# Hash bits on four column quarters, placed by small transfers, in a hash attention kernel

## The chip, the cores and the metric

The kernel runs on one core of a Trainium2 chip. The metric is device microseconds from start to end of one execution of the whole program, the median over several runs. The engines named below are TensorE (PE in the profile, PEld for its weight loads), VectorE (DVE), ScalarE (ACT), GpSimd (POOL) and SyncE (SP, which here only issues transfers).

## The reference

Hash attention over 4 batches x 8 heads, 768 tokens, 64 columns a head, then a feed-forward block. A query sees only the keys whose six hash bits equal its own:

```python
q_bits = (np.einsum('bhsd,dk->bhsk', q, proj) > 0).astype(np.int64)
k_bits = (np.einsum('bhsd,dk->bhsk', k, proj) > 0).astype(np.int64)
q_bucket = np.sum(q_bits * powers, axis=-1)
k_bucket = np.sum(k_bits * powers, axis=-1)
mask = q_bucket[:, :, :, None] == k_bucket[:, :, None, :]
scores = scale * np.matmul(q, k.transpose(0, 1, 3, 2))
scores = np.where(mask, scores, -1000000000.0)
...
attn = attn / (np.sum(attn, axis=-1, keepdims=True) + 1e-09)
return np.matmul(attn, v).astype(np.float32)
...
h = x @ w_in
sp = np.maximum(h, 0.0) + np.log1p(np.exp(-np.abs(h)))
g = h * erf(sp)
return (g @ w_out).astype(np.float32)
```

The feed-forward block has 3072 rows, 512 columns in and out and 2048 inside. All of it is float32.

## The kernel before

The program has two stages: `attention` and `feed_forward`. A third part, `general`, does attention without assumptions on the size of the scores; it is behind a branch at the end and isn't executed with these inputs.

**Pairs, halves, blocks.** Attention works on 16 pairs of heads (`NPAIR`). Two heads of 64 columns fill 128 partitions. `fetch` (L330) brings q, k (transposed, 64 rows a head) and v of a pair with six transfers from SP, into buffers for three pairs. The 768 queries of a pair are two halves of 384 (`HS`). A half `h` has two `score` steps `n`, each over three blocks of 128 keys. One block (L529) is four matmuls for the two heads: 64 rows of bf16 hash signs times hash signs, then 64 rows of float32 k times q, summed in the same bank. The signs of the keys are weighted by 2^100 and a constant row takes the full match off again, so that a pair of tokens with differing bits gets a sum so low that its exponential is 0.

**The signs now.** `hash_bits` (L353) multiplies q and k by the projection: four float32 matmuls of 128 rows by 64 columns, q into partitions 0 to 63 and k into 64 to 127, one pair of matmuls for each half of 384 tokens. The projection `proj_sb` holds head a's six columns at column 0 and head b's at column 32 (`QR`). `sign_bits` (L366) takes the sign with one ACT instruction of 128 x 768, `spread_bits` (L379) writes the weighted key signs twice with DVE, once for each head, with weights that are zero in the other head's rows, and `double_bits` (L390) copies the query signs to the lower partitions with DVE. The tiles `qb` and `kb` have two buffers each. Pair 0 does this in two halves ahead of the loop (`take_bits`, L394).

**After the scores.** `exponential` (L543) goes to ACT, with three buffers in PSUM (`big`) shared by scores and hash bits. `sum_keys` (L590) sums the exponentials over blocks with DVE. `weigh` (L602) multiplies them by v, `divisor` (L635) sums over partitions: four matmuls of 32 columns side by side, 192 columns each. `keep_divisor` (L648) and `leave` (L659) copy both results out with ACT. Then a chain of small transfers on SP inverts and applies the sums, once for each pair: `spread` (zd, L678), `gather` (zc, L685), `invert` with DVE, `ungather` (rd, L703), `widen` (r, two transfers, L713), `normalise` with DVE (L721) and `send` (xs, L727). The tile x, which `leave` writes and `send` reads, has two buffers, and so has the tag that z and r share. On SP one queue takes all of this in order, with the loads of a later pair among it.

Beside that the weights of the feed-forward block are fetched by POOL (L439) and split into float32 with ACT and DVE (L453 to L515), 32 pieces through the whole stage.

**What sets the order.** Each engine executes its instructions in the order in which they are emitted. For attention, `arrange` (L118) makes this order: every step is an `Op` with an engine, an assumed cost in us, a rank, the steps it comes after, and `late`, an assumed delay until other engines see the result. `arrange` plays the steps through with these numbers and takes, at each point, the step that can start first. The order of TensorE is a fixed chain written out by hand (L786 to L793): for each half the next two scores, then, after every even half `h`, the bits of pair `h // 2 + 1`, the divisor of the half before, and two `weigh` steps. The waits themselves follow from which instruction reads or writes which tile.

Of the kernel before, what the change touches and what calls it, by code (L numbers as in the profile page):

```python
# [54 lines left out]
F32 = mybir.dt.float32  # L55
BF16 = mybir.dt.bfloat16
# [7 lines left out]
P = 128  # L64
# [129 lines left out]
def kernel(  # L194
# [33 lines left out]
    misc = ctx.enter_context(tc.tile_pool(name="misc", bufs=1, space=PSUM))  # L228
    small = ctx.enter_context(tc.tile_pool(name="small", bufs=3))
    QR = 32  # L230
    WARM = 7
    proj_sb = const.tile([P, 2 * QR], F32, name="proj_sb")
    weight = const.tile([P, 2], F32, name="weight")
    ones = const.tile([P, D], F32, name="ones")
    sgn = const.tile([P, 1], F32, name="sgn")
    tiny2 = const.tile([P, 1], F32, name="tiny2")
# [18 lines left out]
        )  # L255
    row = const.tile([P, 1], F32, name="row")
    nc.gpsimd.dma_start(out=row, in_=bucket)
    steps = const.tile([P, 5], F32, name="steps")
    for c, (end, factor) in enumerate(
        (  # L260
            (NBIT, NBIT + 1.0),
            (NBIT + 1, -float(NBIT)),
            (QR, -1.0),
            (QR + NBIT, NBIT + 1.0),
            (QR + NBIT + 1, -float(NBIT)),
        )
    ):
        nc.vector.tensor_scalar(
            out=steps[:, c : c + 1],
            in0=row,  # L270
            scalar1=float(end),
            scalar2=factor * BIG,
            op0=ALU.is_lt,
            op1=ALU.mult,
        )
    nc.vector.reduce_sum(out=weight[:, 0:1], in_=steps[:, 0:2], axis=AX.X)
    nc.vector.reduce_sum(out=weight[:, 1:2], in_=steps[:, 2:5], axis=AX.X)
    nc.vector.memset(sgn, -(2.0**-27))
    nc.vector.memset(tiny2, TINY * TINY)
    for j, (c, _) in enumerate(ERF_Q):  # L280
# [72 lines left out]
    def hash_bits(d, big, halves=(0, 1)):  # L353
        if halves[0] == 0:
            d["bits"] = big("bits")
        for half in halves:
            for n, what in enumerate("qk"):
                nc.tensor.matmul(  # L358
                    out=d["bits"][n * D : n * D + D, half, 0:HS],
                    lhsT=proj_sb,  # L360
                    rhs=d[what][:, half * HS : (half + 1) * HS],
                    start=True,
                    stop=True,
                )

    def sign_bits(d, bitp, cols):  # L366

        if cols.start == 0:
            for what in ("qb", "kb"):
                d[what] = bitp.tile([P, S], BF16, name=what, tag=what)  # L370
        nc.scalar.activation(
            out=d["qb"][:, cols].rearrange("p (h s) -> p h s", s=HS),
            in_=d["bits"][:, cols.start // HS : cols.stop // HS, 0:HS],
            func=AF.Sign,
            scale=2.0**100,
            bias=sgn[:, 0:1],
        )
# [12 lines left out]
    def double_bits(d, cols):  # L390

        nc.vector.tensor_copy(out=d["qb"][D:P, cols], in_=d["qb"][0:D, cols])

    def take_bits(d, bitp, halves=(0, 1)):  # L394
        cols = slice(halves[0] * HS, (halves[-1] + 1) * HS)
        sign_bits(d, bitp, cols)
        for ab in (1, 0):
            spread_bits(d, cols, ab)
        double_bits(d, cols)

    def attention():
        NS = NPAIR * 4
        with (
            tc.tile_pool(name="load", bufs=3) as load,
            tc.tile_pool(name="bitp", bufs=2) as bitp,
            tc.tile_pool(name="ep", bufs=1) as ep,
            tc.tile_pool(name="sums", bufs=2) as sums,
            tc.tile_pool(name="xst", bufs=2) as xst,
# [5 lines left out]
            def big(name):  # L414
                return psum.tile([P, 2, 512], F32, name=name, tag="big", bufs=3)

            junk = ep.tile([P, HS], BF16, name="junk")
            NE = 3 * GC
            e_all = ep.tile([P, NE, 2, HS + 1], F32, name="e_all")
# [335 lines left out]
                )  # L755
            for half in range(2):
                hash_bits(pairs[0], big, (half,))
                take_bits(pairs[0], bitp, (half,))

            NH = NPAIR * 2  # L760
            ops = []
# [9 lines left out]
                chain.append((fn.__name__,) + args)  # L771

            def bits_of(i):
                hash_bits(pairs[i], big)

            def sign_of(i):
                sign_bits(pairs[i], bitp, slice(0, S))

            def weigh_bits(i, ab):
                spread_bits(pairs[i], slice(0, S), ab)  # L780

            def copy_bits(i):
                double_bits(pairs[i], slice(0, S))

            chain = []
            order = [("score", 0)]  # L786
            for h in range(NH):
                order += [("score", n) for n in (2 * h + 1, 2 * h + 2) if n < NS]
                if h % 2 == 0 and h // 2 + 1 < NPAIR:
                    order.append(("bits", h // 2 + 1))  # L790
                if h >= 1:
                    order.append(("divisor", h - 1))
                order += [("weigh", 2 * h), ("weigh", 2 * h + 1)]  # L793
            slots = []
            for what, n in order:
                if what == "score":
                    i = n // 4
                    after = tuple(("weigh_bits", i, ab) for ab in range(2)) + (("copy_bits", i),)
                    for c in range(GC):
                        free = (slots[-3],) if len(slots) >= 3 else ()  # L800
                        pe(score, (n, c), 0.82, after + free)
                        slots.append(("exponential", n, c))
                elif what == "bits":
                    pe(bits_of, (n,), 1.34, (("start_pair", n), slots[-3]))
                    slots.append(("sign_of", n))
                elif what == "divisor":
                    pe(divisor, (n,), 0.42, (("sum_keys", n, last_sum(n)), ("keep_divisor", n - 1)))
                else:
                    h = n // 2
                    after = (("exponential", n, GC - 1),)  # L810
                    if n % 2 == 0:
                        after += (("leave", h - 1), ("leave_plain", (h - 1) // 2))
                    pe(weigh, (n,), 2.02, after)
# [40 lines left out]
            for i in range(NPAIR):  # L854
                n = 4 * i
                if i:
                    op(
                        start_pair,
                        (i,),
                        "SP",  # L860
                        3.6,
                        (0, n - 6),
                        (("weigh", n - 9), ("bits_of", i - 1))
                        + tuple(("measure", i - 3, m, half) for m in range(2) for half in range(2)),
                        late=3.5,
                    )
                    op(sign_of, (i,), "ACT", 0.88, (0, n - 2, 9), (("bits_of", i), ("score", n - 5, 2)))
                    for ab in (1, 0):
                        op(weigh_bits, (i, ab), "DVE", 0.43, (0, n - 2, 1), (("sign_of", i),))
                    op(  # L870
                        copy_bits,
                        (i,),
                        "DVE",
                        0.35,
                        (0, n - 2, 2),
                        (("weigh_bits", i, 0), ("weigh_bits", i, 1)),
                    )
                for m in range(2):
                    for half in range(2):
                        op(  # L880
                            measure,
                            (i, m, half),
                            "ACT",
                            0.5,
                            (1, 2 * i + 2, 2 + m, half),
                            (("start_pair", i), ("score", n, 0)),
                        )
                if i == NPAIR - 1:
                    continue
                op(spread, (i,), "SP", 0.4, (0, n, 0), (("keep_divisor", 2 * i + 1),), late=3.0)  # L890
                op(gather, (i,), "SP", 0.35, (0, n, 1), (("spread", i),), late=4.5)
                op(invert, (i,), "DVE", 0.4, (0, n + 8, 3), (("gather", i),))
                op(ungather, (i,), "SP", 0.35, (0, n, 2), (("invert", i),), late=3.0)
                op(
                    widen,
                    (i,),
                    "SP",
                    1.1,
                    (0, n, 3),
                    (("ungather", i), ("send", i - 1)),  # L900
                    late=6.5,
                )
                op(normalise, (i,), "DVE", 0.95, (0, n + 8, 4), (("widen", i), ("leave", 2 * i + 1)))
                op(send, (i,), "SP", 0.35, (0, n, 4), (("normalise", i),), late=2.2)
            for n in range(len(pieces)):
                op(
                    fetch_weights,
# [46 lines left out]
    def general():  # L954

        with (
# [13 lines left out]
            for i in range(NPAIR):  # L970
                d = fetch(i, load)
                b, j = divmod(i, JP)
                hash_bits(d, big)
                take_bits(d, bitp)
                x = ep.tile([P, S], F32, name="x", tag="x")
                for ab in range(2):
                    rows = slice(ab * D, ab * D + D)
# [701 lines left out]
```

## Time and profile before

| | |
|---|---|
| median of 3 runs | 933.58 us (931.9 to 934.86) |
| profiled execution: its own time | 934.86 us |
| profiled execution: its span | 932.9 us |
| mean granted TensorE clock | 0.997 of full |
| instructions | 12993 |
| attention | from the start to about 339 us |
| exponentials, L543, 192 instructions | 149.1 us of ACT, 819 ns each |
| score matmuls, float32, L529 | 156.6 us of PE, 486 ns each, side by side |
| hash bit matmuls, L358, 128 instructions | 51.2 us by single durations, side by side |
| small transfers zd, zc and rd | 6 KB each, 15 or 16 times |
| bytes moved | 80.92 MB, 87 GB/s on the mean |

Span and run time differ by 2 us that lie around the profiled instructions. A float32 matmul shows up as two instructions, one for each pass, and matmuls on different rows or columns of the array run side by side, so that single durations add up to more than the time they take. What a block of matmuls costs is better read from the distance between the starts of neighbouring blocks in the chain of waits.

Idle time of an engine is listed beside the instruction that ended it, with what released it. In the rows of SP (SPq), the times are those of issuing; a row's idle time before it is a wait.

### The profile page before, as it was taken

To read this page: it belongs to the slowest core of one execution; us is meant where nothing else is said; L and a number is where in the kernel's file an instruction comes from. 1 tells how busy PE (TensorE), PEld (TensorE's weight loads), DVE (VectorE), ACT (ScalarE), POOL (GpSimd) and SP (SyncE) were. 2 spreads that over 40 slices of the span, in tenths; PEclk is the share of its full clock that TensorE was granted. 3 is DMA by queue.
4 is the path that set the end of the run, shared out by engine and by line. 5 is a ranking of instruction groups with operands and counts; after the bars stand their busy time and mean duration, and the time that the engine had idled before them with its cause. 6 is when DMAs were issued, how large, how long until landed. Compare 5 with 4: busy or idle time off the path is not lost.

```text
span 932.9 us, 12993 instructions
## 1 busy us (share of the span) xinstructions
PE 916.8 (98%) x5003; PEld 661.9 (71%) x5003; DVE 829.7 (89%) x1041; ACT 771.0 (83%) x1002; POOL 17.4 (2%) x35
## 2 busy tenths in 40 slices
PE   8999999999999999999999999999999999999996
PEld 3444444444444458888888888888888888888885
DVE  4999998999888997899999889998899789988995
ACT  5888787768876838999998998899989997899891
POOL 0000000000000000000000000000000000000000
PEclk9999999999999999999999999999999999999998
DMA  8365455576654322010212012210221111001211
GB/s 198 99 158 147 132 148 139 147 200 165 147 149 131 97 103 97 1 46 34 80 68 79 34 46 69 80 34 34 79 78 36 34 65 49 34 34 46 68 35 48
DMA packets 61398, 80.92 MB, mean 87 GB/s; under 512 B 33296, under 2 KB 46224, under 8 KB 61328
## 3 DMA queue, kind: packets, MB, share of 16 engines
q1 hardware_dynamic: 56672, 64.08, 23.9%
q0 software_dynamic: 4352, 15.73, 5.6%
q8 instruction: 41, 0.67, 0.3%
q10 hardware_dynamic: 304, 0.20, 0.1%
q14 instruction: 29, 0.24, 0.1%
HBM read 64.07 MB, written 15.93 MB: 86 GB/s over the span
## 4 chain that ended last, share of the span: by engine, by line
PE 85%; DVE 7%; DMA 4%; ACT 2%; issue 1%; SPq 0%; DVEq 0%; ACTq 0%
PE M L1238 30%; PE X L1098 27%; PE st L529 11%; PE av L602 9%; PE M L1098 3%; PE bits L358 2%; DMA xs<-x 1%; ACT e_all L543 1%; DVE x_sum L590 1%; PE z_ps L635 1%; DVE x L590 1%; DMA zd<-z 1%; DMA zc<-zd 1%; DVE x L721 1%; DMA r<-rd 1%
## 5 line engine op out<-in xcount | busy, mean ns | idle before, releaser
L1165 DVE SCALAR_TENSOR_TENSOR e<-w,e 128x1024 f32<-128x1024 f32 x144 | 173.4, 1221 | 5.8 <-ACT w L1161 3.0
L1161 ACT ACTIVATE w<-w,cq 128x1024 f32<-128x1024 f32 x144 | 160.7, 1143 | 1.9
L543 ACT ACTIVATE e_all<-st 128x768 f32<-128x768 f32 x192 | 149.1, 819 | 11.3 <-PE st L529 11.3
L529 PE MATMUL st<-q,k 64*128 64x384 f32 x768 | 156.6, 486 | 0.0
L1238 PE MATMUL M<-w_out_sb,h 128*128 128x256 f32 x576 | 140.2, 380 | 0.4 <-DVE h L1180 0.4
L602 PE MATMUL av<-e_all,v 128*64 128x385 f32 (+1 forms) x768 | 131.1, 490 | 0.0
L1098 PE MATMUL X<-x,w_in_sb 128*128 128x256 f32 x512 | 121.2, 380 | 0.0
L1238 PEld LDWEIGHTS M<-w_out_sb,h 128*128 128x128 f32 x576 | 109.3, 190 | 15.9 <-DVE h L1180 1.1
L1098 PEld LDWEIGHTS X<-x,w_in_sb 128*128 128x128 f32 x512 | 97.1, 190 | 13.8 <-ACT h L1116 0.6
L602 PEld LDWEIGHTS av<-e_all,v 128*64 128x64 f32 x768 | 52.4, 136 | 67.2 <-issue 65.4
L1238 PE MATMUL M<-wt,S 128*128 128x256 f32 x384 | 93.4, 379 | 0.4 <-DVE S L1195 0.4
L529 PEld LDWEIGHTS st<-q,k 64*128 64x128 f32 x768 | 69.1, 190 | 32.8 <-issue 32.1
L1098 PE MATMUL X<-x_sum,w_sum 128*128 128x256 f32 x344 | 81.7, 380 | 1.8 <-ACT h L1116 1.8
L1238 PEld LDWEIGHTS M<-wt,S 128*128 128x128 f32 x384 | 72.9, 190 | 10.7 <-DVE S L1195 0.8
L1098 PEld LDWEIGHTS X<-x_sum,w_sum 128*128 128x128 f32 x344 | 65.1, 190 | 12.0 <-ACT h L1116 3.3
L1116 ACT COPY h<-X 128x512 f32<-128x512 f32 x85 | 49.0, 577 | 22.3 <-PE X L1098 21.4
L1142 DVE SCALAR_TENSOR_TENSOR w<-w,e 128x1024 f32<-128x1024 f32 x48 | 58.4, 1221 | 9.6 <-ACT w L1137 9.3
L529 PE MATMUL st<-qb,kb 64*128 64x384 bf16 x384 | 63.7, 327 | 3.3 <-ACT e_all L543 3.2
L1180 DVE TENSOR_TENSOR h<-h,e 128x1024 f32<-128x1024 f32 x48 | 58.0, 1221 | 6.1 <-ACT e L1176 5.9
L659 ACT COPY x<-av 128x384 f32<-128x384 f32 x32 | 15.3, 478 | 57.4 <-DMA xs<-x 28.8
L1156 ACT ACTIVATE w<-e 128x1024 f32<-128x1024 f32 x48 | 50.4, 1050 | 13.3 <-DVE e L1152 13.0
L1152 DVE TENSOR_TENSOR e<-e,w 128x1024 f32<-128x1024 f32 x48 | 57.5, 1219 | 2.7 <-ACT e L1148 2.6
(117 smaller groups left out, 1421.0 us busy)
## 6 DMA issues: line engine op xcount, KB each, us to landing
wt<-wt SPq DMA_DIRECT2D x24, 768.0 KB, 4.3
raw<-in_w_out_dram POOLq DMA_DIRECT2D x16, 512.0 KB, 3.9
raw<-in_w_in_dram POOLq DMA_DIRECT2D x14, 512.0 KB, 4.2
v<-in_v_dram SPq DMA_DIRECT2D x32, 192.0 KB, 4.5
xs<-x SPq DMA_DIRECT2D x16, 384.0 KB, 2.4
q<-in_qkT_dram SPq DMA_DIRECT2D x30, 192.0 KB, 3.4
k<-in_qkT_dram SPq DMA_DIRECT2D x30, 192.0 KB, 4.2
r<-rd SPq DMA_DIRECT2D x30, 192.0 KB, 3.5
```

The costliest lines, as they stand in the source:

```text
L529: nc.tensor.matmul(out=st[:, ab, 0:HS], lhsT=d["k" + src][rows, keys], rhs=d["q" + src][rows, cols], start=(part == 0), stop=(part == 1),)
L543: nc.scalar.activation(out=e[:, :, 0:HS], in_=st[:, :, 0:HS], func=AF.Exp, scale=scale)
L602: nc.tensor.matmul(out=d["av"][rows, 0:w], lhsT=d["v"][:, g * GC + c, rows], rhs=e[:, ab, 0:w], start=(g == 0 and c == 0), stop=(g == 1 an ...
L1098: nc.tensor.matmul(out=d[where][:, u, :], lhsT=a[:, kc, f : f + P], rhs=b[:, kc, :], start=(first and u == 0 and kc == 0), stop=(last and ...
L1116: nc.scalar.copy(out=quarter(p, q), in_=st[p][where])
L1142: nc.vector.scalar_tensor_tensor(out=w, in0=w, scalar=-1.0, in1=st[p]["e", v], op0=ALU.add, op1=ALU.subtract)
L1152: nc.vector.tensor_tensor(out=s, in0=s, in1=st[p].pop(("w", v)), op=ALU.subtract)
L1156: nc.scalar.activation(out=z, in_=st[p]["s", v], func=AF.Square)
L1161: nc.scalar.activation(out=q, in_=z, func=AF.Square, bias=cq[:, j : j + 1])
L1165: nc.vector.scalar_tensor_tensor(out=s, in0=st[p].pop(("q", v, j)), scalar=ERF_Q[j][1], in1=s, op0=ALU.add, op1=ALU.mult,)
L1180: nc.vector.tensor_tensor(out=h, in0=h, in1=st[p].pop(("s", v)), op=ALU.mult)
L1238: nc.tensor.matmul(out=banks[name][:, sub, :], lhsT=a[:, u, sub * P : (sub + 1) * P], rhs=b[:, u, :], start=(c == 0 and k == 0), stop=(c = ...
```

## The change

For pairs 1 to 15 the hash bits are computed by four matmuls of 32 columns side by side (`proj_q`, where head b's columns stand at column 16, `QB`): the two halves of q in partition quarters 0 and 1, those of k in quarters 2 and 3, in one PSUM bank. One ACT instruction of 128 x 384 takes the signs into one tile `sg`, of which there is one. One DVE instruction weights the key half of it. Then eight transfers on SP (`place_bits`), each of 7 rows by 384 columns of bf16, copy the six signs and the constant row of each head and half into `qb` and `kb`, whose other rows are zero. `qb` and `kb` are two fixed buffers each, used in turn; the ones with number 1 are cleared by POOL at the start, those with number 0, which pair 0 fills in the old way, by two POOL steps (`clean`) after pair 0's last score.

In TensorE's chain the bits of a pair move: they come after the scores of odd halves, half a pair earlier than before, and those of pair 1 come right after the second score step. The steps' assumed costs and their conditions change with it. Some small DVE instructions at the start make `proj_q` and the new weights. Pair 0 and `general` keep the old way.

```diff
+    QB = QR // 2
+    proj_q = const.tile([P, QR], F32, name="proj_q")
+    weight_q = const.tile([P, 1], F32, name="weight_q")
...
+    nc.vector.memset(proj_q, 0.0)
+    for ab in range(2):
+        rows = slice(ab * D, ab * D + D)
+        nc.vector.tensor_copy(
+            out=proj_q[rows, ab * QB : ab * QB + NBIT],
+            in_=proj_in[rows, ab * NBIT : (ab + 1) * NBIT],
+        )
+    nc.vector.reduce_sum(out=weight_q, in_=steps[:, 5:8], axis=AX.X)
+    nc.vector.tensor_tensor(out=weight_q, in0=weight_q, in1=weight[:, 0:1], op=ALU.add)
+    nc.vector.tensor_copy(out=weight_q[D + QR : P, :], in_=weight_q[D : D + QR, :])
...
+            sg = bitp.tile([P, HS], BF16, name="sg")
+            spare = {
+                (what, n): bitp.tile([P, S], BF16, name=f"{what}{n}")
+                for n in range(2)
+                for what in ("qb", "kb")
+            }
+            for what in ("qb", "kb"):
+                nc.gpsimd.memset(spare[what, 1], 0.0)
...
             def bits_of(i):
-                hash_bits(pairs[i], big)
+                d = pairs[i]
+                d["bits"] = big("bits")
+                for n, what in enumerate("qk"):
+                    for half in range(2):
+                        row = (2 * n + half) * QR
+                        nc.tensor.matmul(
+                            out=d["bits"][row : row + QR, 0, 0:HS],
+                            lhsT=proj_q,
+                            rhs=d[what][:, half * HS : (half + 1) * HS],
+                            start=True,
+                            stop=True,
+                        )
 
             def sign_of(i):
-                sign_bits(pairs[i], bitp, slice(0, S))
-
-            def weigh_bits(i, ab):
-                spread_bits(pairs[i], slice(0, S), ab)
-
-            def copy_bits(i):
-                double_bits(pairs[i], slice(0, S))
+                nc.scalar.activation(
+                    out=sg,
+                    in_=pairs[i].pop("bits")[:, 0, 0:HS],
+                    func=AF.Sign,
+                    scale=2.0**100,
+                    bias=sgn[:, 0:1],
+                )
+
+            def weigh_bits(i):
+                nc.vector.tensor_scalar(
+                    out=sg[D:P, :],
+                    in0=sg[D:P, :],
+                    scalar1=weight_q[D:P, 0:1],
+                    scalar2=None,
+                    op0=ALU.mult,
+                )
+
+            def place_bits(i):
+                d = pairs[i]
+                for n, what in enumerate(("qb", "kb")):
+                    d[what] = spare[what, i % 2]
+                    for half in range(2):
+                        for ab in range(2):
+                            row = (2 * n + half) * QR + ab * QB
+                            nc.sync.dma_start(
+                                out=d[what][
+                                    ab * D : ab * D + NBIT + 1, half * HS : (half + 1) * HS
+                                ],
+                                in_=sg[row : row + NBIT + 1, :],
+                            )
+
+            def clean(n):
+                nc.gpsimd.memset(spare[("qb", "kb")[n], 0], 0.0)
...
-                if h % 2 == 0 and h // 2 + 1 < NPAIR:
-                    order.append(("bits", h // 2 + 1))
+                if h == 0:
+                    order.insert(2, ("bits", 1))
+                if h % 2 and (h + 3) // 2 < NPAIR:
+                    order.append(("bits", (h + 3) // 2))
...
-                    after = tuple(("weigh_bits", i, ab) for ab in range(2)) + (("copy_bits", i),)
+                    after = (("place_bits", i),)
...
-                    pe(bits_of, (n,), 1.34, (("start_pair", n), slots[-3]))
+                    pe(bits_of, (n,), 0.92, (("start_pair", n), slots[-3]))
...
-                    op(sign_of, (i,), "ACT", 0.88, (0, n - 2, 9), (("bits_of", i), ("score", n - 5, 2)))
-                    for ab in (1, 0):
-                        op(weigh_bits, (i, ab), "DVE", 0.43, (0, n - 2, 1), (("sign_of", i),))
+                    op(sign_of, (i,), "ACT", 0.6, (0, n - 6, 9), (("bits_of", i), ("place_bits", i - 1)))
+                    op(weigh_bits, (i,), "DVE", 0.33, (0, n - 6, 1), (("sign_of", i),))
                     op(
-                        copy_bits,
+                        place_bits,
                         (i,),
-                        "DVE",
-                        0.35,
-                        (0, n - 2, 2),
-                        (("weigh_bits", i, 0), ("weigh_bits", i, 1)),
+                        "SP",
+                        2.7,
+                        (0, n - 6, 2),
+                        (("weigh_bits", i), ("score", n - 5, 2)) + tuple(("clean", m) for m in range(2)) * (i == 2),
+                        late=2.6,
                     )
...
+            for m in range(2):
+                op(clean, (m,), "POOL", 0.7, (0, 0), (("score", 3, 2),), late=0.3)
```

More of the change, by code (lines that the diff above doesn't have):

```diff
@@ L257 @@
     nc.gpsimd.dma_start(out=row, in_=bucket)
-    steps = const.tile([P, 5], F32, name="steps")
+    steps = const.tile([P, 8], F32, name="steps")
     for c, (end, factor) in enumerate(
@@ L265 @@
             (QR + NBIT + 1, -float(NBIT)),
+            (QB, -1.0),
+            (QB + NBIT, NBIT + 1.0),
+            (QB + NBIT + 1, -float(NBIT)),
         )
@@ L364, in hash_bits, with sign_bits @@
                 )
-    def sign_bits(d, bitp, cols):
+    def sign_bits(d, tile_of, cols):
         if cols.start == 0:
             for what in ("qb", "kb"):
-                d[what] = bitp.tile([P, S], BF16, name=what, tag=what)
+                d[what] = tile_of(what)
         nc.scalar.activation(
@@ L392, in double_bits, with take_bits @@
         nc.vector.tensor_copy(out=d["qb"][D:P, cols], in_=d["qb"][0:D, cols])
-    def take_bits(d, bitp, halves=(0, 1)):
+    def take_bits(d, tile_of, halves=(0, 1)):
         cols = slice(halves[0] * HS, (halves[-1] + 1) * HS)
-        sign_bits(d, bitp, cols)
+        sign_bits(d, tile_of, cols)
         for ab in (1, 0):
@@ L404, in attention @@
             tc.tile_pool(name="load", bufs=3) as load,
-            tc.tile_pool(name="bitp", bufs=2) as bitp,
+            tc.tile_pool(name="bitp", bufs=1) as bitp,
             tc.tile_pool(name="ep", bufs=1) as ep,
@@ L757, in attention @@
                 hash_bits(pairs[0], big, (half,))
-                take_bits(pairs[0], bitp, (half,))
+                take_bits(pairs[0], lambda what: spare[what, 0], (half,))
             NH = NPAIR * 2
@@ L973, in general @@
                 hash_bits(d, big)
-                take_bits(d, bitp)
+                take_bits(d, lambda what: bitp.tile([P, S], BF16, name=what, tag=what))
                 x = ep.tile([P, S], F32, name="x", tag="x")
```

## The prediction

> **What bounds the kernel now.** I read the page first, then the chain of waits, then the busy time by stretches, then SP's own queue. The page:
>
> ```profile
> PE 916.8 (98%) x5003; PEld 661.9 (71%) x5003; DVE 829.7 (89%) x1041; ACT 771.0 (83%) x1002; POOL 17.4 (2%) x35
> L659 ACT COPY x<-av 128x384 f32<-128x384 f32 x32 | 15.3, 478 | 57.4 <-DMA xs<-x 28.8
> ```
>
> TensorE is busy 98% of the span, so work taken from it should show. But the copy that empties the attention output (L659) sat idle 28.8 us for the transfer that frees its buffer, so a second loop touches the same stage. The change lies in attention alone (to about 339 us). The early chain there is pure TensorE:
>
> ```profile
> 38.53 1.44 PE bits L358 x8
> 39.97 0.46 PE z_ps L635 x8
> 40.43 4.03 PE av L602 x24
> 44.47 4.95 PE st L529 x36
> ```
>
> Columns: start, length, what. One pair is two blocks of st, av and divisor and one of bits: 2 x (4.95 + 4.03 + 0.46) + 1.44 = 20.32 us. Equal blocks of the chain, the st before a block without bits, stand at 24.14, 44.47 and 125.76 (20.3 us a pair), but from 125.76 to 312.91 nine pairs take 187.2 us, 4.2 over 9 x 20.33. Three stretches of the busy times show where:
>
> ```profile
> 20.00:137.00 117.00, 117.00 (x830) 54.09 (x828) 109.09 (x154) 94.64 (x174) 7.04 (x12) 1.00 0.51 134
> 137.00:296.00 159.00, 155.73 (x1100) 71.87 (x1098) 145.88 (x204) 120.37 (x217) 8.45 (x16) 1.00 0.58 155
> ```
>
> After the times of the stretch come PE, PEld, DVE, ACT and POOL, then the clock (1.00, so no throttle in the sum). PE has no gap to 137 us and 3.3 us of gaps after; DVE is 92 to 93% busy in both. SP's queue in one later pair:
>
> ```profile
> 165.72 0.33 SPq L727 DMA_DIRECT2D xs<-x  x1
> 166.13 1.13 SPq L342 DMA_DIRECT2D q<-in_qkT_dram  x2
> 167.31 1.23 SPq L342 DMA_DIRECT2D k<-in_qkT_dram  x2
> 168.59 1.17 SPq L347 DMA_DIRECT2D v<-in_v_dram  x2
> 169.86 0.58 SPq L678 DMA_DIRECT2D zd<-z  x1
> 173.86 0.33 SPq L685 DMA_DIRECT2D zc<-zd  x1
> 176.68 0.34 SPq L703 DMA_DIRECT2D rd<-zc  x1
> 178.10 1.28 SPq L713 DMA_DIRECT2D r<-rd  x2
> 186.13 0.33 SPq L727 DMA_DIRECT2D xs<-x  x1
> ```
>
> This is one serial loop of 20.4 us: loads 4.1, then 4.0, 2.8 and 1.4 us for three landings with DVE's reciprocal, and 8.0 until DVE has normalised. It runs as long as TensorE's pair, which is why it shows from 137 us on. Its waits there:
>
> ```profile
> SPq L727 <- DVE x L721: 49.4, 8, 7.1
> SPq L685 <- DMA zd<-z: 22.2, 7, 3.4
> SPq L703 <- DVE zc L698: 18.1, 7, 4.0
> ```
>
> 6.2, 3.2 and 2.6 us each: room in which SP could issue something else.
>
> **The change part by part.** (1) **TensorE.** Hash bits were two column halves, each two matmuls side by side over 64 columns; each half runs two f32 passes, the starts 0.32 us apart: 4 x 0.32 + 0.14 of changeover = 1.44. Now all four matmuls, 32 columns each, stand side by side, as the divisor's do: its row has 192 columns in 2 x 0.16 + 0.14 = 0.46. So 384 columns take 2 x 0.32 + 0.14 = 0.79. Gain 0.65 us a pair. From below: if four streams did not overlap better than two, 0; the divisor's row excludes that. From above: bits now stand next to the divisor in the same shape, which may save one 0.14 more. I take 0.65; 15 pairs (the first keeps the old way): 9.7 us.
>
> (2) **ACT and DVE.** These rows carry what goes:
>
> ```profile
> L371 ACT ACTIVATE qb<-bits,sgn 128x768 bf16<-128x768 f32 x15 | 13.5, 901 | 1.6 <-PE bits L358 1.0
> L382 DVE TENSOR_SCALAR kb<-qb,weight 64x768 bf16<-64x768 bf16 x30 | 12.6, 419 | 1.4 <-ACT qb L371 1.0
> L392 DVE COPY qb<-qb 64x768 bf16<-64x768 bf16 x15 | 5.3, 354 | 0.5
> ```
>
> Sign goes from 0.90 to 0.58 (its 384-column form in the first pair), 4.8 us of ACT in all. DVE does one 64x384 multiply (0.32, first pair again) for 2 x 0.42 + 0.35 = 1.19: 0.87 a pair, 13 us. Neither sets the end before 137 us, so there they are worth nothing by themselves; later they shorten the DVE part of the loop by up to 0.87.
>
> (3) **SP.** Eight transfers a pair, 7 rows x 768 bytes, 120 in all. No row is of SBUF to SBUF. The issue is bounded by zc<-zd and xs<-x at 0.33 and by r<-rd at 0.64: 2.6 to 5.1 us. I take 0.58, from zd<-z, the only other transfer of a few rows: 4.6. Landing: 1.4 (rd<-zc) to 4.2 (k). In the queue they wait for weigh_bits on DVE, and behind them stand the loop's own transfers, whose next user is DVE's reciprocal or normalise. New bits stand ahead of the even divisor, ten microseconds earlier than now (49.4 against 60.2 in one pair), and the tile is wanted by the next pair's first scores 17 us later (0.8 + 2 x 4.03 + 2 x 0.46 + 1.5 x 4.95); sign, multiply, issue and landing take some 10, so landing is hidden with about 7 to spare. Issue is hidden if it lies in the 2.6 to 6.2 us waits; ahead of the loads or of zd it would cost all 4.6. As bits of the pair before now come half a period sooner, the loads wait only for their buffers' last readers, so they can be issued ahead of xs<-x, in the 6.2 us wait, as once in the trace (96.05 to 99.7). That would take 4.1 from the serial loop, about what the eight issues may add. I take the loop as unchanged, with bounds of -4 and +4.6 a pair.
>
> The Trainium skill's page "DMA: Bandwidth & Descriptors", section "Anatomy of one DMA — SWDGE (gpsimd) path", speaks against small transfers: some 2.0 us fixed for each, whatever its size. Paid in turn, that would be an estimate of 16 us a pair; the trace has the two r<-rd issued 0.6 apart and both landing after 3.4, so I let fixed costs overlap.
>
> (4) **First pairs and setup.** bits(1) moves ahead of score 2, to about 16.3 us. Its loads were issued at 5.8 to 8.3 and are there. Sign by 18, the multiply behind a 1.76 us sum by 20, issues to 22.6 or 24.6, landing 24.2 to 27.3; score 4 wants it at 26.5 - 0.65. Cost 0 to 1.5 once; I take 1.0. About ten small DVE instructions are new at the start (0.06 to 0.17 each by their like, about 1.1 us); weight was ready at 4.80 and is first used at 8.02: hidden, otherwise up to 1.1. POOL's two cleanings stand by the raw fetches of 27 and 35 us; place_bits(2) comes after 31 and is wanted near 47: nothing, up to a few us once if behind a later fetch.
>
> **Sum.** To 137 us TensorE is the bound: 6 bits blocks x 0.65 = 3.9. The nine later ones (5.9) are half kept, since the loop of 20.4 was the bound about as often as TensorE (PE gaps and chain both): 2.9. Less 1.0 at the start: 5.8 us. From the profiled execution's own 934.86 (span 932.9) this gives 929.1; that execution is the highest of the three, 1.3 above their median, so I forecast 933.58 - 5.8 = 927.8.
>
> **Rivals.** A, TensorE alone: the loads slip into SP's wait, the lighter DVE frees the loop and nothing is given back: 933.6 - 9.7 = 923.9, up to 4.2 less if the present gaps go too (919.7). For it: SP waits 6.2 us for normalise. Against: DVE stays over 90% full.
>
> B, slower: SP's loop becomes the bound. The eight issues, standing ahead of r<-rd and held by weigh_bits, delay normalise; r lands 2.3 us ahead of its use on average by the issue times plus 3.4. Past that point every further us is paid by x's buffer (L659), then by the scores behind it. With 4.6 of issue, less 2.3, less the 0.87 that DVE gains: 1.4 a pair, on the 11 pairs from the fifth on 15 us, less 2 us won in the pairs before: 947; if half of those pairs suffer, 939. For it: the 28.8 us idle at L659. Against: nothing new stands between zd and r if the plan puts the issues behind r.
>
> C, no change: hidden anyway. The loop, not TensorE, is the bound after 137 us and takes back the early gain by pair 10, since it is paced by its own 20.4 us: 933.6 less 0 to 2.
>
> D, four streams overlap no better than two: TensorE gains nothing, SP still pays: 934 to 940. The divisor row is against it.
>
> **How the numbers follow.** Forecast 0.37, A 0.17, B 0.30, C 0.11, D 0.05. A difference under 0.3% (2.8 us) can't be told from none here. Faster: forecast and A, less the forecast's own weak tail (0.02) = 0.52; same: C, that tail and 0.02 of B = 0.15; slower: the rest of B and D = 0.33. The likeliest case's own range is 923 to 931. With A's 920 below and B's half case above, 80% needs 920 to 940.
>
> **What would show it.** Right: bits blocks of 0.75 to 0.85 us on TensorE; a pair of 19.7 us before 137; SP's small issues inside waits; L659's idle no longer than 29 us. Wrong: xs<-x more than 21 us apart pair after pair, st waiting for kb, PE gaps above 8 us after 137, small issues over 0.65 each, or SP standing on weigh_bits with zc or r behind it.

## The result, and the profile after

The changed kernel takes 956.24 us (median of 4 runs, 954.03 to 956.93) against 932.96 for the kernel before on the same chip: a ratio of 1.0243, 95% interval 1.0219 to 1.0268. It is slower by some 23 us, outside the range that was forecast. The profiled execution has a span of 952.2 us (954.03 with what lies around it).

The feed-forward stage is as long as it was: in the chain of waits its first long block of matmuls starts at 339.38 us before and at 358.83 after, 19.45 us later, and the span grew by 19.3. The loss lies in attention. The page after, with the lines that answer to those of the prediction (busy time by engine; the copy that empties the attention output, now L683; the bf16 score matmuls):

```profile
PE 913.8 (96%) x5003; PEld 662.8 (70%) x5003; DVE 822.4 (86%) x1020; ACT 764.4 (80%) x1002; POOL 20.2 (2%) x39
L553 PE MATMUL st<-qb,kb 64*128 64x384 bf16 x384 | 66.2, 335 | 25.7 <-ACT e_all L567 25.0
L683 ACT COPY x<-av 128x384 f32<-128x384 f32 x32 | 15.3, 479 | 85.1 <-DMA xs<-x 63.5
```

The score row before, for comparison:

```profile
L529 PE MATMUL st<-qb,kb 64*128 64x384 bf16 x384 | 63.7, 327 | 3.3 <-ACT e_all L543 3.2
```

TensorE has less to do (916.8 to 913.8 us, and more of it at a lower clock), DVE and ACT too. What grew is waiting: the copy waits 63.5 us for xs instead of 28.8, and the scores wait 25.7 us instead of 3.3, nearly all of it for the exponentials behind that copy. By stretches (the columns as before), the later stretch before and then both after:

```profile
137.00:300.00 163.00, 159.73 (x1130) 73.70 (x1128) 148.55 (x205) 124.37 (x224) 8.45 (x16) 1.00 0.59 156
```

```profile
20.00:137.00 117.00, 109.08 (x778) 51.03 (x778) 99.80 (x134) 83.97 (x156) 8.43 (x14) 0.97 0.52 137
137.00:300.00 163.00, 148.00 (x1054) 69.35 (x1048) 133.30 (x177) 114.12 (x216) 7.39 (x14) 0.97 0.53 142
```

TensorE, DVE and ACT are less busy. TensorE has 22.9 us of gaps instead of 3.3, and they begin well ahead of 137 us. Its clock is 0.97 instead of 1.00, which over these 280 us is, as an estimate, some 8 us more. SP's queue in one pair:

```profile
137.21 0.32 SPq L727 DMA_DIRECT2D rd<-zc  x1
138.71 1.28 SPq L737 DMA_DIRECT2D r<-rd  x2
140.09 3.19 SPq L840 DMA_DIRECT2D qb<-sg  x4
143.38 2.91 SPq L840 DMA_DIRECT2D kb<-sg  x4
146.39 1.16 SPq L358 DMA_DIRECT2D q<-in_qkT_dram  x2
147.60 1.22 SPq L358 DMA_DIRECT2D k<-in_qkT_dram  x2
148.93 1.31 SPq L363 DMA_DIRECT2D v<-in_v_dram  x2
150.35 0.48 SPq L751 DMA_DIRECT2D xs<-x  x1
150.92 0.62 SPq L702 DMA_DIRECT2D zd<-z  x1
154.57 0.34 SPq L709 DMA_DIRECT2D zc<-zd  x1
```

From 140.1 to 151.5 us SP issues with hardly a pause: eight small transfers (6.2 us), six loads (3.9 us), then xs and zd. What this does to the other engines, in the timeline of the same stretch:

```profile
143.76 1.01 DVE L745 SCALAR_TENSOR_TENSOR x<-x,ev,r 128x768 f32<-128x768 f32 x1
...
155.44 0.48 ACT L683 COPY x<-av 128x384 f32<-128x384 f32 x1 [6.54 <-DMA xs<-x]
...
156.68 0.34 PE L553 MATMUL st<-qb,kb 64*128 64x384 bf16 x2 [2.94 <-ACT e_all L567]
...
157.89 0.56 PE L553 MATMUL st<-qb,kb 64*128 64x384 bf16 x2
...
159.49 0.56 PE L553 MATMUL st<-qb,kb 64*128 64x384 bf16 x2
```

DVE has normalised x at 144.77. SP reaches xs 5.6 us later, at 150.35, and the copy that waits for it runs at 155.44. TensorE then stands 2.94 us, and the next blocks of scores start 1.60 us apart (157.89, 159.49) where 0.81 is usual: its granted clock from 156 to 161 us is 0.66. So this gap is paid a second time after it ends. Not every gap is: twelve times the scores waited for exponentials. After five gaps of 0.77 to 1.49 us, and after one of 3.03 us (at 291.66), the next blocks came 0.80 or 0.81 us apart; after the other six, of 1.97 to 3.33 us, distances of 1.12 to 1.60 us followed. The Trainium skill has a rule of this kind ("TensorE: Matmul & The Clock Gate", Part 1): after an idle window of some 3.4 us the array runs at half its clock until it has been busy as long. Here 1.97 us were enough once and 3.03 us were not, so the length of the gap alone does not decide; the measurement goes before the rule.

The mean parts of SP's loop, from distances between starts of these rows from 60 to 300 us, and its period, from the starts of xs from 60 to 320 us (the parts add up to 20.8 and 22.4; loads and small transfers lie in xs to zd or r to xs, where they stand in the order):

| kernel | xs to zd | zd to zc | zc to rd | rd to r | r to xs | period |
|---|---|---|---|---|---|---|
| before | 4.0 | 3.7 | 3.5 | 1.9 | 7.7 | 20.6 |
| after | 1.1 | 3.9 | 3.5 | 1.8 | 12.1 | 22.4 |

### The profile page after: what moved, and what is told of

It reads as the page before. It is cut to its first block, busy times and chain, and to the rows that moved or that the text cites. A ratio compares the mean times of both kernels' runs of the same rounds, so it can differ in the third digit from the quotient of the medians.

```text
span 952.2 us, 13257 instructions
## 1 busy us (share of the span) xinstructions
PE 913.8 (96%) x5003; PEld 662.8 (70%) x5003; DVE 822.4 (86%) x1020; ACT 764.4 (80%) x1002; POOL 20.2 (2%) x39
## 4 chain that ended last, share of the span: by engine, by line
PE 72%; DVE 14%; DMA 9%; ACT 2%; issue 2%; SPq 1%; DVEq 0%; ACTq 0%
PE M L1308 30%; PE X L1168 27%; PE st L553 6%; DVE x_sum L614 5%; PE av L626 5%; DMA xs<-x 4%; PE M L1168 3%; DMA zd<-z 3%; DVE x L614 2%; DMA zc<-zd 2%; ACT e_all L567 1%; DVE x L745 1%; DVE top L513 1%; PE bits L805 1%; DVE rest L531 1%
## 5 line engine op out<-in xcount | busy, mean ns | idle before, releaser
L553 PE MATMUL st<-q,k 64*128 64x384 f32 x768 | 163.4, 503 | 0.0
L553 PEld LDWEIGHTS st<-q,k 64*128 64x128 f32 x768 | 72.2, 195 | 31.3 <-issue 30.2
L553 PE MATMUL st<-qb,kb 64*128 64x384 bf16 x384 | 66.2, 335 | 25.7 <-ACT e_all L567 25.0
L683 ACT COPY x<-av 128x384 f32<-128x384 f32 x32 | 15.3, 479 | 85.1 <-DMA xs<-x 63.5
L553 PEld LDWEIGHTS <-kb 64*128 64x128 bf16 x384 | 22.6, 96 | 73.8 <-issue 48.9
L1186 ACT COPY h<-X 128x512 f32<-128x512 f32 x85 | 49.1, 577 | 22.2 <-PE X L1168 21.3
```

The costliest lines, as they stand in the source:

```text
L553: nc.tensor.matmul(out=st[:, ab, 0:HS], lhsT=d["k" + src][rows, keys], rhs=d["q" + src][rows, cols], start=(part == 0), stop=(part == 1),)
L1186: nc.scalar.copy(out=quarter(p, q), in_=st[p][where])
```

## The experiments

Two theories stood at the start. **Theory 1:** the issue of the eight transfers stands in SP's serial loop, and makes it longer than TensorE's pair. **Theory 2:** the order is the harm: the loads now stand ahead of xs, xs lands behind them, and x's buffer comes late. All kernels of a group ran on the same chip as the kernel before, which had medians of 929.9 to 933.0 there. By the ratio the changed kernel stands at some 953 beside 930. SP's loop is the period by the starts of xs, as above.

| kernel | small transfers a pair | median us | before there | ratio (95%) | SP's loop |
|---|---|---|---|---|---|
| after | 8 on SP | 956.24 | 932.96 | 1.0243 (1.0219 to 1.0268) | 22.4 |
| p16 | 8 on SP, 16 rows | 947.78 | 930.15 | 1.0199 (1.0160 to 1.0237) | 21.9 |
| place_pool | 8 on POOL | 919.07 | 930.15 | 0.9889 (0.9872 to 0.9906) | 19.7 |
| early_bits | none, old hash | 930.29 | 930.15 | 1.0004 (0.9994 to 1.0014) | 20.3 |
| extra_sp | 8 on SP, old hash | 942.12 | 930.15 | 1.0130 (1.0113 to 1.0147) | 21.2 |
| loads_behind | 8 on SP | 943.71 | 929.93 | 1.0143 (1.0126 to 1.0160) | 21.9 |
| half_pool | 4 on SP, 4 on POOL | 937.94 | 929.93 | 1.0070 (1.0048 to 1.0092) | |
| place_act | 8 on ACT | 1005.31 | 929.93 | 1.0805 (1.0786 to 1.0823) | |
| loads_pool | 8 on SP, loads on POOL | 948.83 | 929.93 | 1.0197 (1.0169 to 1.0226) | 22.2 |
| zero_place | none | 918.88 | 930.35 | 0.9869 (0.9844 to 0.9893) | 19.7 |
| four_place | 4 on SP | 933.36 | 930.35 | 1.0037 (1.0020 to 1.0054) | 20.8 |
| p16_behind | 8 on SP, 16 rows | 941.71 | 930.35 | 1.0132 (1.0105 to 1.0159) | 21.3 |
| x_three | 8 on SP | 949.54 | 932.95 | 1.0173 (1.0141 to 1.0204) | 22.4 |
| pool_x_three | 8 on POOL | 919.11 | 932.95 | 0.9858 (0.9834 to 0.9881) | 19.6 |

Of half_pool only the times are used; the profile of four_place is that of the longest of its ten runs (938.75).

### The transfers off SP (place_pool)

```diff
-                            nc.sync.dma_start(
+                            nc.gpsimd.dma_start(
...
                         place_bits,
                         (i,),
-                        "SP",
+                        "POOL",
```

> The changed kernel with the eight small transfers issued by POOL instead of SP; TensorE's chain as in the changed kernel, SP without them, loads still ahead of xs<-x. Theory 1: SP's loop falls to 17 to 18 us of its own, TensorE at 19.7 us a pair sets the time: 920 to 930. Theory 2: xs still lands late, 940 to 950.

919.07 us: just under Theory 1's range, and 11 us under the kernel before. So it is faster than the changed kernel and than the kernel before. TensorE is busy for 279.8 of the 280 us from 20 to 300. Its chain of waits between 60 and 90 us is TensorE alone (start, length, what):

```profile
61.20 4.95 PE st L553 x36
66.15 0.78 PE bits L805 x8
66.93 0.33 PE z_ps L659 x8
67.25 4.02 PE av L626 x24
71.28 4.95 PE st L553 x36
76.23 0.46 PE z_ps L659 x8
```

Bits take 0.78 us, and the divisor behind them 0.33 instead of 0.46. Its rows and those of the bits now name the same shape of the array (128*32); that this is the reason is the reading that fits. A pair takes 19.53 us (67.25 to 86.78 for equal blocks) instead of 20.33. And SP waits again, in 20 to 320 us:

```profile
SPq L702 <- ACT z L672: 36.1, 14, 4.7
...
SPq L751 <- DVE x L745: 24.1, 13, 7.0
```

It waits for zd's and xs's inputs, which it did hardly or not at all with the transfers on it. xs takes 5.5 us to land here (the median from 60 to 310 us; in the changed kernel's pair above it was some 5.1, from 150.35 to the copy at 155.44), and that does no harm: L683 waits 7.0 us for it in all.

### None, and half of them (zero_place, four_place)

```diff
                 for n, what in enumerate(("qb", "kb")):
                     d[what] = spare[what, i % 2]
+                    if i > 1:
+                        continue
                     for half in range(2):
```

In four_place the condition is `if n and i > 1`.

> The changed kernel without the small transfers of pairs 2 to 15: the bits are computed, signed and weighted but not placed, so that from pair 2 on the scores read zeros (or pair 1's bits). All other instructions stand in the same order. Theory 1 in its wider form (SP's loop of a pair is a sum of issues and landings without slack, and the small transfers' issue of 6.2 us is in it in full): the loop is 16 to 17 us of its own, TensorE's 19.5 us a pair is the bound, 917 to 922. A theory that something else of the change (half a pair earlier, one sg tile, loads ahead of xs) makes most of the loss: 935 to 950.

918.88 us, as long as place_pool's 919.07. So of the changed kernel's time, the issue of these transfers from SP is worth the whole 34 us between 953 and 919; the moved bits, the single `sg` tile, the order of the loads and the transfers' own way through memory cost nothing that shows once SP is free of them.

> The same, but of the eight transfers of a pair the four of the queries are issued and the four of the keys left out (the scores read zeros for the keys' bits), POOL as in the changed kernel. Theory 1 as a plain sum: loop 22.5 - 3.1 = 19.4, time 918 to 926. Theory 3 (the room that issue gives up is taken by landings behind the loads, above all that of zd): loop 21 to 22, time 932 to 942.

933.36 us: neither the plain sum (918 to 926) nor all of the loss; in Theory 3's range, whose loop of 21 to 22 it just misses at 20.8 (its parts from 60 to 300 us add up to 21.1). Against zero_place the first four transfers cost 14.5 us, the next four some 20. SP's waits in 60 to 320 us show where the 3.1 us of issue went that it gave up. four_place, then the changed kernel:

```profile
SPq L709 <- DMA zd<-z: 53.8, 13, 5.3
SPq L727 <- DVE zc L722: 41.3, 12, 4.4
```

```profile
SPq L709 <- DMA zd<-z: 39.2, 12, 5.0
SPq L727 <- DVE zc L722: 36.9, 12, 4.1
```

The wait for zd's landing went from 3.3 to 4.1 us each; zd to zc in the loop from 3.9 to 5.4. Issue and landing are not independent terms of a sum.

### Fewer microseconds for each (p16) and another order (loads_behind, p16_behind)

```diff
-                                    ab * D : ab * D + NBIT + 1, half * HS : (half + 1) * HS
+                                    ab * D : ab * D + QB, half * HS : (half + 1) * HS
                                 ],
-                                in_=sg[row : row + NBIT + 1, :],
+                                in_=sg[row : row + QB, :],
```

> The changed kernel, but each of the eight small transfers takes 16 rows (the whole sixteenth of the bits' tile; the nine rows more are zero in the keys) instead of 7. Order of all queues as in the changed kernel. Theory 1 (the eight issues, 0.69 to 0.72 us each with gaps 6.3 us a pair, stand in SP's serial loop and make its 22.5 us): if 16 rows issue in 0.33 to 0.45 the loop loses 2.6 to 3.8 us a pair and the time falls to 920 to 932; if they still take 0.7 it stays at 953 to 959. Theory 2 (the loads now stand ahead of xs<-x, so that xs lands 5 us after its issue instead of 2.4 and x's buffer comes late): xs still lands after 5 us, time 942 to 956.

947.78 us: above what Theory 1 asked for at a shorter issue, and in Theory 2's range. The issue fell to between 0.51 and 0.58 us by 16 rows in place of 7, not to the 0.33 of 128-row transfers; 5.0 us a pair for the eight with their gaps (159.23 to 164.22 in one pair) instead of 6.2. The time fell by some 4 to 5 us (ratio 1.0199 after 1.0243; the intervals overlap, so this step is not clear of noise), less than 15 x 1.2: r to xs shrank by 1.1 us, zd to zc grew by as much (3.9 to 5.0).

```diff
-                        (("weigh", n - 9), ("bits_of", i - 1))
+                        (("weigh", n - 9), ("bits_of", i - 1), ("send", i - 4))
```

> The changed kernel with the loads of a pair put behind xs<-x in SP's order (as in the kernel before); the small transfers stay on SP. Theory 1 (SP's loop is the sum of what SP issues and of the landings that it waits for): the sum stays at 22 to 23 us a pair, 948 to 958 against about 931. Theory 2 (the loads ahead of xs<-x are the harm): xs lands 2.4 us after its issue, L659's copy waits half as long, 934 to 944.

943.71 us lies in Theory 2's range, at its upper end. Putting xs ahead of the loads again is worth about 10 us while the small transfers stay on SP: L683 waits 36 us for xs instead of 63.5. The loop is shorter too, 21.9.

> The changed kernel with 16 rows in each small transfer and with the loads put behind xs<-x, both on SP. Theory 1: 1.2 us of issue a pair less than loads_behind (943.7 against 929.9 there), 930 to 940. Theory 3: zd lands later by what the issue gains, 940 to 945.

941.71: both edits together bring 1 to 2 us more than the order alone, which is inside the intervals; it is in Theory 3's range and under what Theory 1 asked for at its better end. With all issue left on SP, these two gain 11 of the 23 us that were lost.

### The order without the transfers, the transfers without the order (early_bits, extra_sp)

Both start from the kernel before.

```diff
-                if h % 2 == 0 and h // 2 + 1 < NPAIR:
-                    order.append(("bits", h // 2 + 1))
+                if h == 0:
+                    order.insert(2, ("bits", 1))
+                if h % 2 and (h + 3) // 2 < NPAIR:
+                    order.append(("bits", (h + 3) // 2))
...
```

The ranks of sign, weighting and copy move with it (`n - 6` for `n - 2`).

> The kernel before with only the bits moved half a pair earlier in TensorE's chain (as in the change), with its old matmuls, old DVE work and no small transfers; the loads then stand ahead of xs<-x on SP as in the changed kernel. Theory 1: nothing was added to SP, 930 to 936. Theory 2: the order alone brings the late xs: 940 to 952.

930.29 beside 930.15. The order alone, with the loads ahead of xs as in the changed kernel, costs nothing: here SP has to wait for z and x anyway, and the loads are issued in that wait. Theory 2 by itself falls. With the small transfers on SP the order does matter (loads_behind): it is a part of the loss only when SP has no wait left.

```diff
+            sg = ep.tile([P, HS], BF16, name="sg")
+            nc.gpsimd.memset(sg, 0.0)
...
+            def extra(i):
+                for n in range(2):
+                    for half in range(2):
+                        for ab in range(2):
+                            row = (2 * n + half) * QR + ab * QR // 2
+                            nc.sync.dma_start(
+                                out=sg[row + 8 : row + 9 + NBIT, :],
+                                in_=sg[row : row + NBIT + 1, :],
+                            )
...
+                if i >= 2:
+                    op(extra, (i,), "SP", 2.7, (0, n - 6, 2), (("divisor", 2 * i - 4),), late=2.6)
```

> The kernel before, its hash as it was, with eight transfers of 7 rows by 384 bf16 a pair added on SP for pairs 2 to 15, after the divisor of the half in which the changed kernel has its own; nobody waits for what they move. Theory 1: 6 us a pair on SP, part of it in waits: 942 to 955. Theory 2: the loads mostly stay behind xs<-x, so 932 to 937.

942.12: 12 us slower for transfers that nobody waits for, at 0.69 us of issue each. The changed kernel is 23 us over the kernel before; the 34 above count from 919, with TensorE's gain of 11. That extra_sp loses less than 23 fits its order: the eight stand partly in SP's wait for x (r to xs stays at 7.8), and the loads mostly after xs.

### Other queues (half_pool, place_act, loads_pool)

half_pool splits `place_bits` into queries on SP and keys on POOL; place_act and loads_pool change the queue of the eight transfers and of `start_pair` as place_pool does above.

> The changed kernel with the four transfers of the keys' bits on POOL and the four of the queries' on SP. Theory 1: SP loses 3.1 us a pair, its loop of 19.4 is as long as TensorE's pair of 19.5, time 918 to 926. A theory in which any small transfer on SP's queue disturbs it as a whole: 935 to 945.

937.94 (median of five runs of 934.4 to 948.7; the ratio, which leaves the longest out, puts it at some 936). It lies in the second range. With 4 transfers on SP the plain sum fails here as in four_place (933.36), where the loop's other parts took room back; for half_pool itself this is not shown.

> The changed kernel with the eight small transfers issued by ACT. Theory 1 read for ACT: 8 x 0.7 to 0.8 us of issue come on top of some 16.8 us that ACT is busy in a pair of 19.5: 22.4 to 23 us, so ACT becomes the bound, 948 to 962. If issue time only hurts a queue that waits in turn for landings: 920 to 930.

1005.31, worse than the range. ACT has 0.72 us for each issue, and what stands behind the eight in its queue waits until they are out (timeline of DVE, then of ACT):

```profile
136.10 0.32 DVE L824 TENSOR_SCALAR sg<-sg,weight_q 64x384 bf16<-64x384 bf16 x1
```

```profile
135.88 0.72 ACTq L840 DMA_DIRECT2D qb<-sg  x1
136.64 0.71 ACTq L840 DMA_DIRECT2D qb<-sg  x1
137.40 2.00 ACTq L840 DMA_DIRECT2D qb<-sg  x2
139.58 3.14 ACTq L840 DMA_DIRECT2D kb<-sg  x4
142.76 0.48 ACT L683 COPY x<-av 128x384 f32<-128x384 f32 x1 [5.80 <-DMA kb<-sg]
```

The 5.80 us ahead of the copy are issuing, not a wait for inputs: the weighted bits are ready at 136.42, and in all 15 pairs they were ready before the first transfer of the keys. From the first issue to the end of the last, the eight took 6.1 to 10.3 us in a pair, 7.8 on the mean, where the expectation had 5.6 to 6.4. And it left out what a stop of ACT does to TensorE: the scores stood 60.5 us for exponentials, and the granted clock was 0.91 from 20 to 137 us and 0.90 from 137 to 300. Why some issues took longer than 0.72 us is open.

> The changed kernel with the loads of q, k and v of pairs 2 to 15 on POOL and the eight small transfers still on SP. Theory 1: SP loses 3.9 us of its 22.5, 18.6 is under TensorE's 19.5, so 917 to 926 although the small transfers are where they were; a theory in which the small transfers themselves (their landings, the data path) do the harm: 940 to 955.

948.83: Theory 1 as a plain sum of issues falls here. The second range holds it, but not its theory: in place_pool the same small transfers land by the same way, and the time is 919. SP got rid of 3.9 us and the loop stayed at 22.2. SP now waits: rd to r takes 5.1 us instead of 1.8 and zc to rd 6.3 instead of 3.5, and DVE stood 32.8 us in 11 waits for r, against 1.3 before this edit. The loads, issued by POOL at other times, are under way when rd and r should land. That they collide with them is the reading that fits; no run separates it from POOL's own waits. The eight transfers still stand between r and xs, which takes 8.2 us.

### The door (x_three, pool_x_three)

```diff
+                if what == "x" and i % 3 == 2 and i < 12:
+                    return w_out_sb[:, 14:16, :].rearrange("p f t -> p (f t)")[:, 0:S]
                 if i < NPAIR - 1:
                     return xst.tile([P, S], F32, name=what, tag="x" if what == "x" else "z")
```

> The changed kernel with a third buffer for x up to pair 11 (in a part of w_out_sb that is filled only later), the eight transfers on SP as they were. If two x buffers are what makes the late xs<-x cost time: L683 waits no longer and the time falls to 925 to 935. If the loop on SP is the bound by its own length (22.5 us a pair, whatever frees x): L683's wait shrinks, others (the divisor's copy, the loads) take its place, 945 to 955.

949.54, the second case. L683's (now L685's) wait for xs fell from 63.5 to 4.0 us:

```profile
ACT x L685 <- DMA xs<-x: 4.0, 1, 4.0
```

The loop stayed at 22.4 us, and TensorE's gaps spread over other waits. So x's two buffers are only the door by which the long loop was felt first. What the third buffer did bring, ratio 1.0243 to 1.0173, goes with the clock: the mean granted clock is 0.997 instead of 0.988, and the scores' longest wait for exponentials is 1.9 us instead of 3.3.

> The kernel with the eight transfers on POOL and the third buffer for x. TensorE is the bound there at 19.5 us a pair and L683 waited only 7 us for xs: 915 to 920 against about 930 before.

919.11, the same as place_pool within the intervals of both. Where TensorE is the bound, the buffer is worth nothing.

## Why the prediction was wrong

**What bounds the kernel: right.** SP's loop of 20.4 us beside TensorE's 20.3 was the picture, and it held: 0, 4 and 8 transfers on SP give 918.9, 933.4 and some 953.

**TensorE's gain: right, a little small.** 0.65 us a pair were taken; 1.44 + 0.46 became 0.78 + 0.33, a gain of 0.79. With SP free this is 11 us of the 930 (place_pool), near the 9.7 of case A and under its 923.9.

**"I take the loop as unchanged": the step that failed.** The prediction set 4.6 us of new issue against 4.1 us of loads moved into SP's wait for x, and took the difference as nothing. By the table of the loop, r to xs grew by 4.4 us, xs to zd shrank by 2.9 only, and the other three parts changed by 0.1 together: the loop became 1.5 us longer by its parts, 1.8 by its period. Two terms of the sum had the wrong size.

First the issue: the term was 0.58 us each, 4.6 a pair, bounded by 2.6 and 5.1. The profile after has

```profile
L840 SPq DMA_DIRECT2D qb<-sg x60: 688/722/1342, 17.0 to 321.8; - x60
L840 SPq DMA_DIRECT2D kb<-sg x60: 688/689/700, 21.9 to 324.8; - x60
```

(nanoseconds, least, median and most, in the answer on the tile `sg`), with some 0.07 us between two: 6.2 a pair, above the upper bound. No row of before was a transfer within the on-chip memory of 7 rows, and the nearest row (zd, 0.58) was taken as if the next one up, r's 0.64, closed the range.

Second, what the loads set free. Right behind the loads, the issue of xs itself took longer (in place_pool, where SP waits between the loads and xs, its median is 0.34). Before and after:

```profile
L727 SPq DMA_DIRECT2D xs<-x x12: 320/326/339, 61.1 to 289.4; - x12
```

```profile
L751 SPq DMA_DIRECT2D xs<-x x13: 383/746/2253, 60.5 to 325.6; - x13
```

One wait had to take both. Small transfers and loads did go between r and xs, as in the listing above: 6.2 + 3.9 = 10.1 us, in a wait of 6.2. By the prediction's own sizes it would have been 8.7, of which 2.5 stick out, less than the 4.1 won elsewhere; by the measured ones 3.9 or more stick out and 2.9 are won. The loop has no wait for x left. early_bits and extra_sp show that each of the two alone costs nothing or 12 us; the changed kernel has both.

The size of the issue is not all of it. p16 has 5.0 us of issue, inside the bounds, and its loop is still 21.9, because zd to zc takes 5.0 us there. The sum held zd's landing fixed, and it is not; what delays it was not separated.

The measured 1.5 to 1.8 us lie inside the bounds of -4 and +4.6 that the prediction gave for the loop, but the range of 920 to 940 did not carry the upper one: 1.8 us on 15 pairs are 27. In attention 19.4 were measured, as not all pairs had the long period (the last starts of zd are 20.8 and 21.0 us apart). TensorE's pair was won and then not used.

**The rivals.** B had the mechanism and the sign (SP's loop becomes the bound, 947 or 939) and got 0.30. It expected the small transfers ahead of r; they stood behind r, which the text counted as evidence against B. Behind r they delay xs instead, and xs is a link of the loop as well. C and D: four streams do overlap (0.78), and nothing was hidden anyway.

**Costs at nothing that were nothing, or little.** Landing of the small transfers: the scores waited 3.0 us in all for qb's, and zero_place and place_pool agree to 0.2 us without and with them. The 16 us a pair for fixed costs paid in turn did not show either: on POOL the eight landed after 3.6 us at the median, and a pair took 19.53. The start (1.0 us in the sum), the new DVE work and POOL's cleanings were not tried alone; TensorE's gain of 15 x 0.79 = 11.9 us against place_pool's 11.1 leaves, as an estimate, about 1 us for all of them.

**Not foreseen:** that gaps can cost clock, and that issue time given back does not come back in full (p16, four_place), as zd to zc then takes longer.

## What to carry to other kernels

A queue that waits for its own transfers in turn is a loop; write its period down term by term, and before a transfer is put on it, subtract from each wait everything that the edit sends there, not each item by itself. The same transfers cost 34 us on the queue that carries the critical loop and nothing that shows on POOL's (953 and 919, and 919 without them), so a price for a transfer belongs to a queue, not to the transfer. When a price isn't in the trace, the nearest rows are no upper bound unless one of them is clearly worse than the case.

## What the runs showed of the hardware

- Issue from SP took 0.69 to 0.72 us for 7 rows of 768 bytes within the on-chip memory, 0.51 to 0.58 for 16 rows, against 0.33 for 128 rows to or from DRAM in the kernel before; from ACT mostly 0.72 for 7 rows, from POOL 0.50. Behind six loads the issue of xs, 128 rows, took 0.75 at the median and up to 2.25.
- After a gap of 2.94 us TensorE ran scores at 1.60 us a block instead of 0.81, with a granted clock of 0.66 over 5 us. A gap of 1.97 us was followed by the same (0.66 from 225 to 230 us), one of 3.03 us by none of it (1.00 from 291.6 to 296.6).
- The divisor's block took 0.33 us in the chain of waits behind a block of the same shape of the array, and 0.46 behind the scores.
- The Trainium skill's "DMA: Bandwidth & Descriptors" ("Issuing engines are not separate DMA queues") says that issuing from several engines saves only the time to initiate, which is usually small beside the transfer. Here this time is 6.2 us a pair, and moving it was worth 34 us; the measurement decides.
